# Three VectorE sums of x issued ahead of the weighting of v, with GpSimd busy beside them

## Chip, cores, metric

One core of a Trainium2 chip. The metric is device time in microseconds (us); lower is better.

## The reference

A linear ("performer") attention over eight batches, followed by a gated feed-forward layer, fp32 in and out:

```python
h = proj - sq; h = h - np.max(h, axis=-1, keepdims=True); phi = np.exp(h) / np.sqrt(m)
kv  = np.einsum('bhsm,bhsd->bhmd', k_p, v)          # with z = sum of k_p
num = np.einsum('bhsm,bhmd->bhsd', q_p, kv)         # attention = num / den
out = gelu(x @ w_gate) * (x @ w_val) @ w_out        # x: the attention, 4608 tokens x 512
```

## The kernel before

Each engine's instruction order is written by hand. While TensorE works on the feed-forward layer of one tile of 512 tokens, the attention of a later batch is prepared. The product with `w_val` uses seven products of half size in place of eight. It needs four sums of halves of the transposed x per tile (`ts`; they are coded as subtractions and called sums here). `v` multiplies v by weights that stand in for the subtracted maximum, in two halves; `kz` then multiplies k by it.

```python
def ts(self, n, eng):                      # class Gated; sum n of a token tile
    # ... cut: views b[row half, token half] of x, and t = x_sums
    p, q = ((b[0, 1], b[0, 0]), (b[1, 1], t[:, 0]), (b[1, 1], b[0, 1]), (b[1, 0], t[:, 1]))[n]
    eng.tensor_sub(t[:, n], p, q)          # two SBUF inputs, 128x512 bf16

def v(self, half, eng):                    # class Attention
    # ... cut: views
    eng.tensor_mul(vev[:, isl, :, :D], vfv[:, isl],
                   wkv[:, isl].unsqueeze(3).broadcast_to((P, NI // 2, 2, D)))   # two SBUF inputs, fp32
    eng.tensor_copy(vev[:, isl, :, D], wkv[:, isl])
```

The stretch in question (h is token tile 1, counted from zero; m is batch 2; n is batch 1):

```python
h.ts(0, nc.gpsimd)                                               # sum 0, on GpSimd
# ... cut
n.nx(4)
h.ga(0, 1)
after(load_kq("k", 3) + load_kq("q", 3) + load_v(3))             # three DMA issues, on GpSimd
m.qf(3, True)
h.ts(2, nc.vector)                                               # sum 2
m.qx(3)
h.vm(0, 1); h.vs(0, 1, act); m.kx(4); h.vm(0, 5)                 # P1, P5 on TensorE
h.ts(1, nc.vector)                                               # sum 1
m.v(1, pool)                                                     # v1, on GpSimd
m.v(0, nc.vector)                                                # v0
h.ga(6, 0); h.vm(0, 6); h.ga(6, 1)                               # P6
h.ts(3, nc.vector)                                               # sum 3
# ... cut: copies of ScalarE
h.vm(0, 7); h.va(0, 2); h.vm(0, 2)                               # P7, the addition that reads it, P2
h.gp(7, 0, 2); h.gp(7, 2, 4)
h.vm(0, 3); h.va(0, 1); h.vm(0, 4); h.va(0, 0)                   # P3, P4
h.ge(6)
m.kz(0, False); m.kz(1)                                          # kz, 72 small matmuls
```

The softmax here doesn't subtract the row's maximum and nothing guards it: scores larger than these inputs give would overflow.

## Time and profile before

| | before |
|---|---|
| time, median of 3 | 343.86 us (343.67 to 344.12) |
| TensorE busy | 96% of the span |
| TensorE idle, 68 to 75.3 us of the trace | 2.35 us |
| sum 3 on VectorE | 2.99 us, against 0.42 for its form |

TensorE sets the time, so what counts is the hole in its row near 73 us. The prediction shows the lines that carry this. The traces do not reach this stretch at the same time: sum 0 starts between 67.11 and 68.46 us, for reasons that lie ahead of the change (the traced run of the kernel before took 344.6 us). So I measure with D, the time from the start of sum 0 on GpSimd to the start of the tile product behind kz: before, 76.54 - 68.46 = 8.08 us.

### The profile page before, as it was taken

The numbers are of one execution on the slowest core, as the hardware profiler recorded it, in microseconds if no ns is written. First come the engines' busy times: TensorE is split into PE (matmuls) and PEld (weight loads), VectorE is DVE, ScalarE is ACT, GpSimd is POOL, SyncE is SP. The second block draws the span as 40 slices with busy tenths as digits, with TensorE's granted clock in tenths as the row PEclk, the third lists the DMA queues.
The fourth block names the chain that finished last, engine by engine and source line by source line (L and its number), as shares of the span: only waits on it lengthen the run. The fifth ranks groups of instructions, "written<-read, shape, count | busy, mean of one in ns | idle before, by whom it ended". The sixth has DMA issues, their size and how long they took to land.

```text
span 342.8 us, 7993 instructions
## 1 busy us (share of the span) xinstructions
PE 327.5 (96%) x3114; PEld 206.4 (60%) x3155; DVE 230.3 (67%) x479; ACT 214.3 (63%) x434; POOL 152.5 (44%) x154
## 2 busy tenths in 40 slices
PE   7889999879999999999999999999999999999994
PEld 3565455556645664476546654665476786686683
DVE  2975388879783759366836774567457677796783
ACT  3894366755687568756776577657765546626640
POOL 8326004073467446745594459476968400000000
PEclk9999999999999999999999999999999999999998
DMA  8999999599969454965298519772413041014004
GB/s 155 277 206 207 207 251 198 149 166 233 188 94 335 78 104 65 324 119 107 33 300 154 114 18 267 196 106 35 92 34 61 10 101 25 1 30 94 2 0 123
DMA packets 67173, 45.08 MB, mean 131 GB/s; under 512 B 47296, under 2 KB 60096, under 8 KB 67136
## 3 DMA queue, kind: packets, MB, share of 16 engines
q0 software_dynamic: 14848, 22.12, 31.3%
q1 hardware_dynamic: 51744, 21.64, 30.4%
q10 hardware_dynamic: 544, 0.82, 0.8%
q8 instruction: 24, 0.39, 0.5%
q14 instruction: 13, 0.11, 0.1%
HBM read 37.78 MB, written 9.44 MB: 138 GB/s over the span
## 4 chain that ended last, share of the span: by engine, by line
PE 83%; DVE 6%; DMA 3%; ACT 3%; issue 3%; POOL 2%; DVEq 0%; POOLq 0%
PE g_ps L433 20%; PE o_ps L559 17%; PE val_one L378 11%; PE val_two L378 9%; PE out_one L533 5%; PE out_two L533 3%; PE v_ps L462 3%; PE g_ps L425 3%; PE kz_ps L285 3%; DMA q_in<-in_q_dram 3%; PE nd L302 2%; PE pk L220 2%; DVE x_sb L314 2%; PE pq L242 2%; DVE val_c L387 1%
## 5 line engine op out<-in xcount | busy, mean ns | idle before, releaser
L433 PE MATMUL g_ps<-xT,w_gate_sb 128*128 128x512 bf16 x352 | 108.2, 379 | 0.5
L440 ACT ACTIVATE g_gelu<-g_ps 128x512 bf16<-128x512 f32 x108 | 63.6, 597 | 54.1 <-PE g_ps L433 25.3
L559 PE MATMUL o_ps<-w_out_sb,gated 128*128 128x512 bf16 x275 | 64.6, 380 | 1.1 <-issue 0.6
L480 POOL TENSOR_TENSOR gated<-g_gelu,val_c 128x512 bf16<-128x512 bf16 x29 | 33.7, 1164 | 50.8 <-DVE iden L313 26.2
L387 DVE TENSOR_TENSOR val_c<-val_one,val_c 128x256 f32<-128x256 f32 x48 | 20.3, 424 | 48.6 <-ACT g_gelu L440 39.6
L378 PEld LDWEIGHTS <-w_val_sb 128*128 128x128 bf16 x384 | 36.5, 98 | 18.3 <-issue 2.3
L559 PEld LDWEIGHTS <-gated 128*128 128x128 bf16 x288 | 26.5, 98 | 33.5 <-issue 3.9
L383 ACT COPY val_c<-val_one 128x256 f32<-128x256 f32 x95 | 35.2, 371 | 12.4 <-PE val_one L378 9.3
L249 ACT ACTIVATE q_pT<-pq 128x512 bf16<-128x512 f32 (+1 forms) x68 | 34.6, 598 | 11.9 <-PE pq L242 11.7
L378 PEld LDWEIGHTS <-val_sums 128*128 128x128 bf16 x288 | 27.3, 98 | 24.3 <-DVE x_sb L314 3.6
L233 DVE TENSOR_REDUCE nmax<-pk 128x8 f32<-128x1024 f32 (+2 forms) x43 | 39.7, 968 | 3.1 <-PE pk L220 1.2
L433 PEld LDWEIGHTS <-w_gate_sb 128*128 128x128 bf16 x376 | 34.9, 98 | 11.2
L378 PE MATMUL val_one<-x_sums,w_val_sb 128*128 128x256 bf16 x192 | 36.6, 273 | 1.7 <-DVE val_c L387 1.7
L228 ACT ACTIVATE k_p<-pk 128x1024 bf16<-128x1024 f32 (+2 forms) x43 | 33.0, 832 | 8.3 <-PE pk L220 6.7
L271 POOL TENSOR_TENSOR v_ext<-vf,wk 128x1152 bf16<-128x1152 f32 x13 | 30.3, 2334 | 14.0 <-ACT wk L260 14.0
L387 DVE TENSOR_TENSOR val_c<-val_two,val_c 128x256 f32<-128x256 f32 x96 | 36.0, 413 | 0.8 <-PE val_two L378 0.8
L484 POOL TENSOR_TENSOR gated<-g_gelu,val_c 128x256 bf16<-128x256 bf16 x34 | 24.2, 712 | 15.0 <-ACT g_gelu L440 15.0
L314 DVE TENSOR_TENSOR x_sb<-nd,iden 128x512 bf16<-128x512 f32 (+2 forms) x41 | 27.7, 676 | 1.4
L564 DVE COPY o_sb<-o_ps 128x512 f32<-128x512 f32 x20 | 13.7, 685 | 19.4 <-PE o_ps L559 14.9
L383 ACT COPY val_c<-val_two 128x256 f32<-128x256 f32 x45 | 16.8, 373 | 11.6 <-PE val_two L378 11.6
L484 DVE TENSOR_TENSOR gated<-g_gelu,val_one 128x256 bf16<-128x256 bf16 x48 | 20.0, 416 | 6.0 <-ACT g_gelu L440 5.7
L378 PE MATMUL val_two<-x_sums,val_sums 128*128 128x256 bf16 x96 | 18.4, 274 | 1.0 <-POOL x_sums L455 0.3
(104 smaller groups left out, 488.3 us busy)
## 6 DMA issues: line engine op xcount, KB each, us to landing
out_dram<-o_sb SPq DMA_DIRECT2D x67, 128.0 KB, 3.3
vf<-in_v_dram POOLq DMA_DIRECT2D x7, 1152.0 KB, 12.0
q_in<-in_q_dram POOLq DMA_DIRECT2D x8, 576.0 KB, 9.4
k_in<-in_k_dram POOLq DMA_DIRECT2D x7, 576.0 KB, 6.1
w_gate_sb<-in_moe_w_gate_dram POOLq DMA_DIRECT2D x3, 512.0 KB, 18.2
w_val_sb<-in_moe_w_val_dram POOLq DMA_DIRECT2D x3, 512.0 KB, 19.8
w_out_sb<-in_moe_w_out_dram POOLq DMA_DIRECT2D x3, 512.0 KB, 13.2
vf<-in_v_dram SPq DMA_DIRECT2D x1, 1152.0 KB, 5.7
```

What stands on the lines that cost most here:

```text
L228: last["begun"] = nc.scalar.activation(self.k_p[:, gs, i0:i0 + n, :], pk, func=Exp)
L233: nc.vector.reduce_max(self.nmax[:, gs, i0:i0 + n], pk, axis=AX, negate=True)
L249: last["begun"] = nc.scalar.activation(dst[:, a, i0:i0 + n], self.pq[c][a].rearrange("m (i e p) -> m i e p", e=2, p=SP), func=Exp)
L314: nc.vector.tensor_mul(x_sb[:n].rearrange("p (g h d) -> p g h d", g=2, h=4)[:, gs], ndv[:, :, :, :D], iden[:n, gs].broadcast_to((n, gs.sto ...
L378: nc.tensor.matmul(ps, w[:, c, self.i * P:(self.i + 1) * P], x[:, c], start=first and c == 0, stop=c == 1, skip_group_check=not first)
L383: copy(self.c[:, {1: 0, 6: 1, 5: 2}[n]], self.beta if n == 5 else self.one)
L387: nc.vector.tensor_add(part, (self.gamma, self.beta, self.one)[k], part)
L433: last["begun"] = nc.tensor.matmul(self.gps[jf], w_gate_sb[:, jm, jf * P:(jf + 1) * P], x_tiles[self.t][:, jm], start=(jm == 0), stop=(jm ...
L440: nc.scalar.activation(self.gelus[jf][:, part], src, func=Gelu)
L480: eng.tensor_mul(self.gated[:, i, :], self.gelus[i], self.v[i].row())
L484: eng.tensor_mul(self.gated[:, i + HF, ts], self.gelus[i + HF][:, ts], s.c[:, 2] if half else s.one)
L559: nc.tensor.matmul(self.ps[qq], self.g.gated[:, f, qq * P:(qq + 1) * P], w_out_sb[:, f, :], start=(jf == 0), stop=(jf == N_DFF - 1))
```

## The change

The intent: sum 3 loses 2.5 us behind v1. Issued ahead of v0 it would be through before v1 begins, and what waits for it would move up. No instruction is added or taken away.

```diff
         m.qf(3, True)
-        h.ts(2, nc.vector)
         m.qx(3)
 ...
         h.ts(1, nc.vector)
+        h.ts(2, nc.vector)
+        h.ts(3, nc.vector)
         m.v(1, pool)
         m.v(0, nc.vector)
         h.ga(6, 0)
         h.vm(0, 6)
         h.ga(6, 1)
-        h.ts(3, nc.vector)
```

## The prediction

> **Names.** Sum n is `h.ts(n)`, one 128x512 bf16 addition of halves of the transposed x of token tile 1 (counted from zero) into `x_sums`. Sum 0 runs on GpSimd, sums 1, 2 and 3 on VectorE. v0 and v1 are the halves of the weighting of v of batch 2, `m.v(0)` on VectorE and `m.v(1)` on GpSimd, each a multiply (line 271) and a small cast (line 273). P1 to P7 are the seven products `h.vm(0, n)` of TensorE. kz is `m.kz`, 72 small matmuls that read v0 in their first half and v1 in their second.
>
> **What bounds the kernel now.** First the page: the share of each engine, and the chain that ended last.
>
> ```profile
> PE 327.5 (96%) x3114; PEld 206.4 (60%) x3155; DVE 230.3 (67%) x479; ACT 214.3 (63%) x434; POOL 152.5 (44%) x154
> PE 83%; DVE 6%; DMA 3%; ACT 3%; issue 3%; POOL 2%; DVEq 0%; POOLq 0%
> ```
>
> TensorE is busy for 96% of the span and is 83% of the chain. So a change on VectorE is worth only what it takes out of a gap of TensorE. The next view, busy time by stretch, shows whether there is such a gap where the change works (columns: stretch, its length, busy time and instructions of PE, PEld, DVE, ACT, POOL, granted clock, DMA).
>
> ```profile
> core 0: us, PE busy (x) PEld busy (x) DVE busy (x) ACT busy (x) POOL busy (x), PEclk, DMA share, GB/s
> 68.00:75.30 7.30, 4.95 (x34) 2.87 (x36) 6.10 (x9) 4.34 (x8) 6.24 (x6) 1.00 0.85 139
> 75.30:94.00 18.70, 18.51 (x226) 12.96 (x230) 15.06 (x39) 9.82 (x22) 7.14 (x8) 1.00 1.09 214
> ```
>
> From 68 to 75.3 us TensorE misses 2.35 of 7.30 us; after that it misses 0.19 of 18.7. The chain of waits puts the largest hole behind sum 3:
>
> ```profile
> 71.73 0.26 DVE x_sums L455
> 71.99 2.51 issue
> 74.50 0.42 DVE val_c L387
> ```
>
> "issue" here is not real issue time: the timeline, in order of time (start, duration, engine, line, what, idle before and releaser), shows sum 3 lasting through it.
>
> ```profile
> 68.42 0.43 DVE L455 TENSOR_TENSOR x_sums<-xT 128x512 bf16<-128x512 bf16 x1 [0.16 <-DMA xT<-x_sb]
> 68.46 1.40 POOL L455 TENSOR_TENSOR x_sums<-xT 128x512 bf16<-128x512 bf16 x1 [10.55 <-DMA xT<-x_sb]
> 69.89 0.42 DVE L455 TENSOR_TENSOR x_sums<-xT,x_sums 128x512 bf16<-128x512 bf16 x1 [1.04 <-POOL x_sums L455]
> 70.23 1.35 DVE L271 TENSOR_TENSOR v_ext<-vf,wk 128x1152 bf16<-128x1152 f32 x1
> 71.58 2.99 DVE L455 TENSOR_TENSOR x_sums<-xT,x_sums 128x512 bf16<-128x512 bf16 x1
> 72.10 2.19 POOL L271 TENSOR_TENSOR v_ext<-vf,wk 128x1152 bf16<-128x1152 f32 x1
> 72.90 0.38 PE L378 MATMUL val_two<-xT,val_sums 128*128 128x256 bf16 x2
> 74.20 0.49 POOL L273 CAST v_ext<-wk 128x18 bf16<-128x18 f32 x1
> 74.50 0.41 DVE L387 TENSOR_TENSOR val_c<-val_one,val_c 128x256 f32<-128x256 f32 x1
> 74.97 0.38 PE L378 MATMUL val_one<-x_sums,w_val_sb 128*128 128x256 bf16 x2 [1.68 <-DVE val_c L387]
> 75.28 1.33 PE L285 MATMUL kz_ps<-v_ext,k_p 64*128 64x65 bf16 x72
> 76.54 0.39 PE L378 MATMUL val_one<-xT,w_val_sb 128*128 128x256 bf16 x2
> ```
>
> In order: sums 2, 0, 1, v0, sum 3 and v1; P3 at 72.90; the addition that reads P7 at 74.50; P4 at 74.97; kz; the next tile product at 76.54. Sum 3 takes 2.99 us, a sum of its form 0.42 (median of six). It stays open while v1 runs on GpSimd and ends 0.28 after v1's multiply does. Behind it in VectorE's queue stands the addition that P4 waits for (it frees the accumulator), and P4 stands in front of kz. So TensorE loses 1.68 us to a VectorE instruction whose own work is 0.4 us.
>
> **What the Trainium skill says.** "SBUF — State Buffer", section "Who interferes with whom": a VectorE instruction with two SBUF inputs contends with a GpSimd instruction that reads SBUF, as an exclusive lock; whoever issues first keeps it, and the other blocks for the whole instruction. The trace agrees in both directions: v1 blocks sum 3 (2.99 against 0.42), and sum 2, at 68.42, delays sum 0 on GpSimd (1.40 against a median of 1.15). The same pair v0/v1 of batch 1 collides the other way round, with VectorE first:
>
> ```profile
> 54.33 1.36 DVE L271 TENSOR_TENSOR v_ext<-vf,wk 128x1152 bf16<-128x1152 f32 x1
> 54.38 3.32 POOL L271 TENSOR_TENSOR v_ext<-vf,wk 128x1152 bf16<-128x1152 f32 x1 [10.93 <-ACT wk L260]
> 57.65 0.26 POOL L273 CAST v_ext<-wk 128x18 bf16<-128x18 f32 x1
> 18.68 0.75 PE L285 MATMUL kz_ps<-v_ext,k_p 64*128 64x65 bf16 x36 [0.23 <-POOL v_ext L273]
> ```
>
> GpSimd ends its multiply 2.01 us after VectorE's ends (57.70 less 55.69) and its cast 2.22 after. The VectorE cast in between took its usual 0.23. The last line, of batch 0, shows that the second half of kz waits for GpSimd alone, 36 matmuls after the first half had gone.[...] "Perfetto Trace Analysis", section "GPSIMD Engine Instruction", calls GpSimd spans unreliable. That fits: sum 3, free to begin at about 71.75, was already shut out although v1 is drawn from 72.10. So I take ends and spacings of GpSimd, not starts, as measures.
>
> **The change part by part.** The instruction order of the two kernels differs on VectorE alone: sum 2, sum 1, v0, sum 3 becomes sum 1, sum 2, sum 3, v0. Nothing is added or removed, and no engine gets more work. On TensorE one wait is new, of P7 for sum 2 (before it was covered by the wait for sum 1).
>
> (a) Sum 0 is no longer delayed: 1.40 becomes 1.15, so it ends at 69.61, not 69.86. The three DMA issues of GpSimd and v1 behind them come 0.25 earlier, v1 drawn from 71.85.
>
> (b) VectorE's sum 1 waits for sum 0 and starts 0.03 later, at 69.64; the place of sum 2 before it is now idle. Sums follow each other at 0.34 (69.89 to 70.23): sum 2 at 69.98, sum 3 at 70.32, v0 at 70.66. All three sums run while GpSimd only issues DMAs; sum 1 and v0 did so before without delay. v0 ends at 70.66 + 1.36 = 72.02, its cast at 72.16. P7 needs sum 2 at 71.55 and it is there at 70.4. P6 at 70.71 stays where it is, since a copy of ScalarE (70.28 + 0.38) releases it.
>
> (c) v1 asks for the lock while v0 holds it. By the spacing of batch 1 its cast ends 2.22 after 72.02, at 74.24, in place of 74.69.
>
> (d) The addition no longer stands behind a blocked sum 3. P7 is done at 71.93, the cast at 72.16, so the addition runs to about 72.55. P4 then needs no wait: it follows P3 at the usual 0.22, at 73.12. The first half of kz follows 0.31 later (74.97 to 75.28 before), at 73.43, and takes half of the 1.26 from 75.28 to 76.54, to 74.06. The second half needs v1: 74.24 + 0.06 = 74.30, and ends 0.63 later, at 74.93.
>
> (e) The next product starts at 74.93 in place of 76.54: 1.61 us saved. Without (a) it would be 0.25 less, 1.36.
>
> From there TensorE has 0.19 us of gaps up to 94 us, and each later step repeats at 35.46 us (pk at 129.22, 164.69, 200.15 in the chain). Its helpers wait for TensorE, not for a clock, so the saving should reach the end. I take 1.5 us, between the two sums: 343.86 - 1.5 = 342.4 us, or 0.4%.
>
> **Rivals.** First, the lock goes to v1 before v0: sum 3 was shut out 0.35 before v1's drawn start, so v1 claims early. Then v0 would be blocked until about 74.0, end at 75.4, and the addition, P4 and kz follow it: P4 at about 76, kz's end at about 77.5, some 1.0 us slower, 344.9. Against it: v0 starts at 70.66, and GpSimd still has its last DMA issue to begin at 71.08; before, v0 started at 70.23 in the same phase untouched. One in ten.
>
> Second, the wait for v1 takes the place of the wait for the addition, and all of kz waits for it: 74.30 + 1.26 = 75.56, a saving of 0.98, 342.9. Against it stands the batch 0 line above, and in the instruction list only the first matmul of the second half carries a wait for GpSimd.
>
> Third, the saving is given back at a transfer: loads for batch 3 and transposes of k do not get earlier by the same amount. The transposes of k are issued at 80.51 and land 7.0 later, at 87.5; the first reader runs at 93.74. That leaves 6 us, so I expect no loss. If it happened, 343.9.
>
> Fourth, new collisions of two-input VectorE work with GpSimd after 75 us, because the engines' phases move. They all follow TensorE, so their relative order should stay; I allow 0.3 us.
>
> **Range and chances.** The two sums give 342.25 and 342.5. The second rival and part losses reach 342.9 to 343.3, and little speaks for more than 1.9 us of gain, since the whole gap is 2.35. Before's three runs spread by 0.45. So 341.9 to 343.3 should hold eight times in ten, with the first rival outside it. Two per cent is 6.9 us, nearly three times the gap: within 2% is 0.98, and 0.01 each for faster and slower.
>
> **What would show each step.** (a) sum 0 near 1.15. (b) three VectorE sums of 0.42 in a row, then v0 of 1.36. (c) v1 lengthened, ending about 2.0 after v0. (d) P4 right behind P3, and kz in two pieces with a wait of some 0.2 for GpSimd. (e) the product after kz near 74.9, then 1.5 less at every later landmark, such as pk at 129.22. Wrong would be: v0 longer than 2 us, kz in one piece behind v1, or a landmark difference that shrinks between 75 and 130.

## The result, and the profile after

| | before | after |
|---|---|---|
| median, 4 runs each | 343.98 us | 345.68 us (345.17 to 346.27) |
| ratio | | 1.0051 (1.0032 to 1.0071) |
| D | 8.08 us | 8.84 us |
| TensorE idle, 68 to 75.3 us | 2.35 us | 2.68 us |

It is slower by 0.5%, within 2%, and outside the predicted range. The page's shares, then busy time by stretch:

```profile
PE 327.5 (95%) x3114; PEld 205.8 (60%) x3155; DVE 230.8 (67%) x479; ACT 214.3 (62%) x434; POOL 153.1 (45%) x154
PE 81%; DVE 8%; DMA 3%; issue 3%; ACT 2%; POOL 1%; SPq 0%; DVEq 0%; POOLq 0%
```

```profile
68.00:75.30 7.30, 4.62 (x32) 2.63 (x29) 6.23 (x7) 4.34 (x8) 6.80 (x6) 1.00 0.91 169
75.30:94.00 18.70, 18.51 (x221) 12.79 (x224) 15.06 (x40) 9.64 (x22) 7.14 (x8) 1.00 0.98 201
```

VectorE's share of the chain went from 6% to 8%; the hole in TensorE grew, and the stretch after it is as full as before. In the chain, "issue" now stands behind v0 in place of sum 3:

```profile
70.17 1.25 DVE v_ext L271
71.42 3.19 issue
```

The timeline of the changed kernel (start, duration, engine, line, what, idle before and releaser):

```profile
67.89 1.15 POOL L455 TENSOR_TENSOR x_sums<-xT 128x512 bf16<-128x512 bf16 x1 [10.50 <-DMA xT<-x_sb]
69.41 0.42 DVE L455 TENSOR_TENSOR x_sums<-xT 128x512 bf16<-128x512 bf16 x1
69.75 0.42 DVE L455 TENSOR_TENSOR x_sums<-xT,x_sums 128x512 bf16<-128x512 bf16 x1
70.08 4.61 DVE L271 TENSOR_TENSOR v_ext<-vf,wk 128x1152 bf16<-128x1152 f32 x1
71.28 2.19 POOL L271 TENSOR_TENSOR v_ext<-vf,wk 128x1152 bf16<-128x1152 f32 x1
73.39 1.42 POOL L273 CAST v_ext<-wk 128x18 bf16<-128x18 f32 x1
74.69 0.41 DVE L387 TENSOR_TENSOR val_c<-val_one,val_c 128x256 f32<-128x256 f32 x1
75.15 0.38 PE L378 MATMUL val_one<-x_sums,w_val_sb 128*128 128x256 bf16 x2 [2.44 <-DVE val_c L387]
75.46 1.33 PE L285 MATMUL kz_ps<-v_ext,k_p 64*128 64x65 bf16 x72
76.73 0.39 PE L378 MATMUL val_one<-xT,w_val_sb 128*128 128x256 bf16 x2
```

Sum 0 takes 1.15 and the sums 0.42, as predicted. But v0 takes 4.61 us in place of 1.36. It is drawn from 70.08 and ends 1.22 us after v1's multiply does (74.69 and 73.47), so most of its own 1.36 us ran only when v1 had done. v1 took the lock although it is drawn as starting 1.2 us after v0. The short sum 3, which v1 used to hold up, cost 0.28 us after v1's end; the long v0, with its cast, costs 1.22. GpSimd's cast is then caught by v0 in turn (1.42; undisturbed it takes 0.26). P4 waits 2.44 us, before 1.68.

Counted from the start of sum 0, D is 0.76 us longer; the time rose by 1.7. So a second cost had to be found.

A small part of it stands in this trace. Counted in the same way, the later landmarks lie 0.75 us behind those before up to pk at 164.87 us (before 164.69), but 1.04 behind at 200.62 (before 200.15). In the step between, an addition of VectorE waits 1.94 us, where it waits 1.58 in the four other steps that have it and in all five of the kernel before; the kernel before first, then the changed one:

```profile
180.01 0.42 DVE L387 TENSOR_TENSOR val_c<-val_one,val_c 128x256 f32<-128x256 f32 x1 [1.58 <-PE val_one L378]
180.55 0.43 DVE L387 TENSOR_TENSOR val_c<-val_one,val_c 128x256 f32<-128x256 f32 x1 [1.94 <-PE val_one L378]
```

The trace names no cause for these 0.29 us. They recur in after_again, e2, e3, e5 and e8 below, and as 0.38 in an earlier step of e4; the one trace of the kernel before, e1, e6 and e7 do not have them. Whether they belong to the change is not shown.

### The profile page after: what moved, and what is told of

Read it like the earlier page. It is cut to its first block, busy times and chain, and to the rows that moved or that the text cites. A ratio compares the mean times of both kernels' runs of the same rounds, so it can differ in the third digit from the quotient of the medians.

```text
span 343.3 us, 7994 instructions
## 1 busy us (share of the span) xinstructions
PE 327.5 (95%) x3114; PEld 205.8 (60%) x3155; DVE 230.8 (67%) x479; ACT 214.3 (62%) x434; POOL 153.1 (45%) x154
## 4 chain that ended last, share of the span: by engine, by line
PE 81%; DVE 8%; DMA 3%; issue 3%; ACT 2%; POOL 1%; SPq 0%; DVEq 0%; POOLq 0%
PE g_ps L433 20%; PE o_ps L559 16%; PE val_one L378 11%; PE val_two L378 9%; PE out_one L533 5%; PE out_two L533 3%; PE v_ps L462 3%; PE g_ps L425 3%; PE kz_ps L285 3%; DVE nmax L233 2%; PE nd L302 2%; PE pk L220 2%; DVE x_sb L314 2%; DMA kT<-k_in 2%; PE pq L242 2%
```

## The experiments

Nine runs; each kernel gave a correct result.

**after_again**: the changed kernel unaltered, for its time and clock.

> The changed kernel once more, for its time and to see whether its trace repeats. D is the time from the start of sum 0 on GpSimd to the start of the tile product behind kz: 8.08 us in the kernel before (68.46 to 76.54), 8.84 in the changed one (67.89 to 76.73). Theory (v1 claims the shared lock ahead of v0): D again 8.8, v0 again about 4.6 us long, time 0.8 to 1.7 us above the kernel before. Rival (the slower time comes from elsewhere, a later stage or the granted clock): D again 8.8, but the difference of the times well over 0.8, with a lower clock or a later landmark that drifts apart.

Measured: 346.06 us median of 6 (345.2 to 346.57) against 344.13, ratio 1.0056 (1.0043 to 1.0068). v0 is 4.62, D is 76.65 - 67.79 = 8.86. Its profiled run had a mean clock of 0.993; the first trace of the changed kernel had 1.0. Busy time by stretch shows where (the first number behind the POOL column is the granted clock):

```profile
76.00:77.00 1.00, 1.00 (x48) 0.87 (x41) 0.24 (x1) 0.00 (x0) 0.00 (x0) 0.84 1.69 88
77.00:78.00 1.00, 1.00 (x8) 0.70 (x6) 0.79 (x2) 0.71 (x2) 0.00 (x0) 0.50 1.08 172
78.00:79.00 1.00, 1.00 (x12) 0.80 (x11) 0.85 (x3) 0.66 (x2) 0.00 (x0) 0.50 1.21 242
79.00:80.00 1.00, 1.00 (x3) 0.30 (x2) 0.71 (x2) 0.37 (x1) 0.00 (x0) 0.50 1.07 426
```

For about 3.4 us (76.7 to 80.1) after the longer hole, TensorE runs at half clock. The chain of waits shows what that costs at the first matmuls of the next step, first in the changed kernel's first trace, then in this one:

```profile
93.99 0.78 PE pk L220 x24
```

```profile
95.34 0.78 PE pk L220 x24
```

From the start of sum 0 that is 26.10 and 27.55 us, so 1.45 us for the low clock; the kernel before has 93.81 - 68.46 = 25.35. The changed kernel's ten runs spread accordingly: the four with a mean clock of 1.0 took 345.17 to 345.39, the six with 0.992 to 0.995 took 345.74 to 346.57. The kernel before is not free of this: 3 of its 29 runs with a recorded clock had 0.993 and took 345.20 to 345.84, against about 344.1 for the others. None of these three was traced. Both theories of the expectation have a part: the lock (v0, D) and the clock.

**e1_sum2_early**: half of the change.

```diff
+        h.ts(2, nc.vector)      # ahead of m.qx(3), as before the change
 ...
         h.ts(1, nc.vector)
-        h.ts(2, nc.vector)
         h.ts(3, nc.vector)
```

> Only half of the change: sum 2 stays ahead of sum 1, as before, sum 3 goes ahead of v0. v0 then begins some 0.7 us after the end of sum 0 in place of 1.1. Theory (v1 claims the lock between 0.75 and 1.1 us after sum 0 has ended): v0 gets the lock first, takes 1.36, v1 ends about 2.0 after it, D 6.4 to 6.8, time 1.3 us below the kernel before. Rival (v1 claims the lock at once when sum 0 has ended, and single sums slip in between): v0 is blocked as in the changed kernel, about 4.6 us long, D about 8.8 to 9.1, time 0.8 us above.

Measured: 346.07 us against 344.13, ratio 1.0055 (1.0038 to 1.0073). The expectation missed: v0 was not let in first. Already sum 3 was shut out:

```profile
69.43 4.23 DVE L455 TENSOR_TENSOR x_sums<-xT,x_sums 128x512 bf16<-128x512 bf16 x1
```

Sum 3 reads what sum 1 writes, and is drawn 0.46 us after sum 1, not 0.34. That is 1.89 us after the start of sum 0 (67.54). In the changed kernel a sum drawn 1.86 us after it (69.75 - 67.89) was let through. Counted from the end of sum 0 the order would be the reverse (blocked at 0.49, let through at 0.71), because sum 0 takes 1.40 here; so I count from its start. D is 9.55, and the clock fell to 0.50 in this trace too.

**e3_v1_waits_v0**: the order on the lock is forced.

```diff
-        m.v(1, pool)
-        m.v(0, nc.vector)
+        v0 = m.v(0, nc.vector)
+        v1 = m.v(1, pool)
+        behind(v0[0], v1[:1])     # v1's multiply waits for v0's multiply
```

> The changed kernel with one more wait: v1 on GpSimd waits for the end of v0's multiply on VectorE, so that the order of the two on the lock is forced as the prediction assumed it. Theory (only who gets the lock first was wrong in the prediction): v0 1.36 us, v1 ends 2.0 to 2.2 later, kz in two pieces, D 6.5, time 1.3 to 1.6 us below the kernel before. Rival (GpSimd's DMA issues, not v1, block v0): v0 still over 2 us, until the third issue ends, D 7.5 or more.

Measured: 342.80 us median of 5 (342.14 to 343.13) against 344.13, ratio 0.9963 (0.9951 to 0.9975). Its timeline:

```profile
69.31 1.35 DVE L271 TENSOR_TENSOR v_ext<-vf,wk 128x1152 bf16<-128x1152 f32 x1
70.75 2.15 POOL L271 TENSOR_TENSOR v_ext<-vf,wk 128x1152 bf16<-128x1152 f32 x1 [0.24 <-DVE v_ext L271]
72.09 0.75 PE L285 MATMUL kz_ps<-v_ext,k_p 64*128 64x65 bf16 x36
73.16 0.76 PE L285 MATMUL kz_ps<-v_ext,k_p 64*128 64x65 bf16 x36 [0.32 <-POOL v_ext L273]
```

v0 takes 1.35, v1 ends 2.24 after it, kz goes in two pieces with a wait of 0.32, and D is 73.85 - 67.11 = 6.74: the predicted course, with 1.3 us gained. The DMA issues of GpSimd alongside v0 did not disturb it.

**e6_probe**: when is the lock taken? Fourteen tiny additions with two SBUF inputs stand behind sum 1.

```diff
         h.ts(1, nc.vector)
+        probe(14)        # 14 x nc.vector.tensor_add, 128x4 bf16, SBUF inputs
         h.ts(2, nc.vector)
```

> The changed kernel with 14 additions of 128x4 with two SBUF inputs between sum 1 and sum 2 on VectorE, as a probe of when the lock is taken (result unchanged, time not of interest). Theory: the probes run at their own pace, 0.1 to 0.2 us each, until some 0.75 to 1.1 us after the end of sum 0, and then one of them lasts until v1's multiply has ended, 2.5 us or more, although v1 is drawn as starting a microsecond later. Rival (only long operations are shut out, or the lock is taken when v1 is drawn as starting): all probes before v1's drawn start are short.

Measured: one look, 347.33 us, not of interest. Five probes follow each other at 0.07 us. The sixth:

```profile
69.90 3.73 DVE L137 TENSOR_TENSOR probe_sb<-still 128x4 bf16<-128x4 bf16 x1
```

It is drawn 1.88 us after the start of sum 0 (68.02) and 0.73 after sum 0's end, and ends when v1's multiply does (73.60). v1's multiply itself is drawn only from 71.41. So the lock was gone 1.5 us before the drawn start, and an operation of four elements per partition is shut out like a long one. Together with the runs above: let through at 1.86, blocked at 1.88 and 1.89. Here that is about when the first of three DMA issues ends (69.92); in e1 sum 3 was shut out 0.26 us before that (69.43, the issue ends at 69.69), so the end of an issue is not the mark.

**e4_v1_on_vector**: nothing on GpSimd that reads SBUF beside v0.

```diff
-        m.v(1, pool)
         m.v(0, nc.vector)
 ...
         h.va(0, 2)
+        m.v(1, nc.vector)
```

> The changed kernel with v1 moved from GpSimd to VectorE, behind v0 and the first addition: nothing on GpSimd then reads SBUF while v0 runs, though its three DMA issues stay where they were. Theory (v1's early claim of the lock, and nothing else of GpSimd, blocks v0): v0 1.36 us, v1 1.36, D 6.2 to 6.3, 1.7 to 1.9 us below the kernel before, some 0.4 faster than the kernel with the forced wait. Rival (descriptor generation itself blocks long two-input operations of VectorE): v0 over 2 us, D 7 or more.

Measured: 342.67 us (342.22 to 342.97) against 344.30, ratio 0.9949 (0.9935 to 0.9964). v0 and v1 take 1.35 each, D is 73.81 - 67.56 = 6.25, and kz goes in one piece at 72.54. So it is v1 on GpSimd, not the DMA issues alone, that blocks v0. Both this kernel and e3 beat the two kernels. By D this one is 0.5 us ahead of e3, but the intervals of their times overlap.

**e8_after_filled**: the changed kernel with TensorE's hole filled.

```diff
         h.va(0, 1)                        # cut: kz then keeps this accumulator
+        m.kz_ps = two_banks("kz_ps", False)
+        for _ in range(10): nc.tensor.matmul(m.kz_ps[0][0], still[:, :P], still)
         h.vm(0, 4)
```

> The changed kernel with ten dummy matmuls of 128x512 in TensorE's gap ahead of P4, written into the accumulator of kz, which kz then overwrites. Theory (the slower ones of the changed kernel's runs come from the granted clock, which falls to 0.50 for 3 to 4 us after the longer gap): the clock stays at 1.00 from 75 to 84 us, D about 8.8 to 9.0, and all runs lie at 345.0 to 345.5, none near 346.4; median 1.1 us above the kernel before. Rival (the two groups of runs have another cause): the runs still fall into two groups 1 us apart, median 1.7 above.

Measured: 345.38 us median of 6 (344.75 to 345.63) against 344.30, ratio 1.0025 (1.0010 to 1.0040). D is 8.84, so the lock costs as much as ever, but no run lies near 346.4, all six have a mean clock of 0.998 or more, and the clock stays up in the trace:

```profile
77.00:78.00 1.00, 1.00 (x22) 0.72 (x15) 0.71 (x2) 0.40 (x2) 0.00 (x0) 1.00 2.16 126
78.00:79.00 1.00, 0.96 (x14) 0.67 (x13) 1.00 (x4) 1.00 (x3) 0.00 (x0) 1.00 0.72 116
```

Useless matmuls made the changed kernel faster, by 0.31% in the two ratios (1.0056 to 1.0025), or 1.1 us. What is left, 0.25% or 0.9 us (0.3 to 1.4), fits the 0.76 us that D grew by and the 0.29 lost later.

**e7_probe_two_issues**: the probe kernel with one DMA issue fewer between sum 0 and v1.

```diff
-        after(load_kq("k", 3) + load_kq("q", 3) + load_v(3))
+        after(load_kq("k", 3) + load_kq("q", 3) + load_v(3, nc.sync))
```

> The probe kernel with the load of v for batch 3 issued from SyncE, so that two DMA issues, not three, stand between sum 0 and v1 on GpSimd (time not of interest). Sums and probes so far fit one moment of the claim, 1.87 us after the start of sum 0 (let through at 1.86, blocked at 1.88 and 1.89). Theory A[...]: the first blocked operation starts about 0.5 to 0.75 us earlier, 1.1 to 1.4 after the start of sum 0. Theory B (the claim comes a fixed time after sum 0, whatever stands between): a probe at about 1.88 is the first blocked. In both the blocked one ends with v1's multiply, now 0.75 us earlier.

Measured: one look, 347.29 us, not of interest. Sum 1, 1.19 us after the start of sum 0 (67.94), goes through; the very first probe, at 1.53, is blocked:

```profile
69.47 3.33 DVE L137 TENSOR_TENSOR probe_sb<-still 128x4 bf16<-128x4 bf16 x1
```

So the claim comes between 1.19 and 1.53, 0.33 to 0.69 us earlier for one issue fewer. Theory B is out. A's direction holds, but the blocked probe lies outside the 1.1 to 1.4 that it named (the claim itself may lie inside), and the step per issue is smaller than an issue's drawn 0.75 us.

**e2_sum2_late**: the other half of the change.

```diff
         h.ts(1, nc.vector)
         h.ts(2, nc.vector)
-        h.ts(3, nc.vector)
 ...
         h.ga(6, 1)
+        h.ts(3, nc.vector)
```

> The other half of the change: sum 2 goes behind sum 1, but sum 3 stays behind v0 as before. v0 is then drawn from 1.86 us after the start of sum 0, just ahead of the claim at 1.87. Theory (claim at 1.87 us): v0 gets the lock by a hair, 1.36 us, sum 3 is blocked as in the kernel before, D 7.9 to 8.1, time within 0.3 us of the kernel before. If v0 loses by a hair: v0 about 4.6, D 9.0 or more, time 1 to 2 us above.

Measured: 344.54 us against 344.30, ratio 1.0003 (0.9987 to 1.0019). v0 got in by a hair, 1.86 us after the start of sum 0:

```profile
69.78 1.36 DVE L271 TENSOR_TENSOR v_ext<-vf,wk 128x1152 bf16<-128x1152 f32 x1
```

Sum 3 was then blocked as in the kernel before (2.66 us), and D is 75.75 - 67.92 = 7.83. The claim time found from the other runs foretold this. D is 0.25 us shorter and the time is not, since this trace too loses 0.29 us between 165 and 200 us.

**e5_loads_behind_v1**: no DMA issue between sum 0 and v1.

```diff
-        after(load_kq("k", 3) + load_kq("q", 3) + load_v(3))
+        begun3 = last["begun"]
 ...
         m.v(1, pool)
+        behind(begun3, load_kq("k", 3) + load_kq("q", 3) + load_v(3))
         m.v(0, nc.vector)
```

> The changed kernel with the three DMA issues for batch 3 moved behind v1 on GpSimd, so that v1 follows sum 0 directly. Theory[...]: with no issue between, the claim comes at once after sum 0 and lasts only v1's own time; the blocked VectorE operation (sum 1 or sum 2) takes 2.2 to 2.7 us, not 4.2 to 4.6, v0 is free with 1.36, D 7.8 to 8.2, time within 0.4 us of the kernel before. Rival (the length of the block has nothing to do with the issues): the blocked operation still takes over 4 us and D is 9 or more.

Measured: 344.29 us against 344.04, ratio 1.0001 (0.9969 to 1.0033). v1 now follows sum 0 directly and catches sum 1, for 2.35 us in place of 4.2 to 4.6; v0 takes 1.35. D is 75.34 - 67.75 = 7.59, a little under the expected 7.8. So the length of the block depends on the issues that v1 has ahead of it.

## Why the prediction was wrong

**What bounds the kernel: right.** TensorE, with a hole behind a blocked VectorE operation. Its stretch from 75.3 to 94 us stayed equally full, and in the first trace the later landmarks carried the difference on, with 0.29 us added between 165 and 200 us.

**(a) and the sums of (b): right.** Sum 0 took 1.15, all three sums 0.42, and P6 and P7 found them ready. For sum 3 this was luck: it came 1.86 us after the start of sum 0, and in the probe run an operation at 1.88 was shut out.

**v0 in step (b), with (c): the step that failed.** I let v0 start at 70.66 "untouched" because GpSimd still had its last DMA issue to begin at 71.08. That took the claim to come after the last issue. The runs put it about 1.87 us after the start of sum 0, near the end of the first of three issues. In the prediction's own frame that is 68.46 + 1.87 = 70.33, and v0 came at 70.66. v1's lead over its drawn start, which I read off sum 3 as "0.35", was only a lower bound: sum 3 had merely been the first to knock. The probe shows 1.5 us. My counter-evidence, the v0 before at 70.23, fitted because it lay 1.77 us after sum 0's start, 0.1 us ahead of the claim.

**(d) and (e): wrong as a consequence, right once v0 goes first.** With the forced wait P4 follows P3 directly, kz splits and 1.3 us are gained, against 1.5 predicted. D is 6.74 where I had 6.47 (74.93 - 68.46). So the mechanism of the gain was right and the winner of the lock wrong.

**The first rival happened, and I gave it one in ten.** Its size was near for the lock alone: D of 9.04 by its numbers (77.5 - 68.46), measured 8.84. Its 344.9 missed the clock.

**The clock was in no step and no rival.** The hole grew to 2.44 us, and in six of ten runs the mean clock was lower; in the one of them that was traced TensorE ran at 0.50 for about 3.4 us, which cost 1.45 us. "TensorE: Matmul & The Clock Gate" (the Trainium skill), section "What's actually happening", gives a window of 3413 ns that runs freely and lets the clock fall after an idle window. The length of the low phase agrees, and a free-running window fits that only some runs are hit. In the clock records of the packed traces the low phase lasts 3.413 us in all four traces that have one, and the full clock before it lasted 71.68 us in two and 68.27 in two, which are 21 and 20 such lengths. But a hole of 2.45 us, shorter than the window, was enough in after_again, and one of 2.44 in the first trace was not. Filling the hole removed the slow group (none of six runs, against six of ten), so the cause is shown.

**The sum.** 0.76 us from the lock, 0.29 from the later wait, and 1.45 in six of ten runs (0.87 on average) give an estimate of 1.9; measured were 1.7 and 1.9 in the two comparisons. The 0.29 has no shown cause.

**Still open.** Why v1 claims that early. "Perfetto Trace Analysis" (the Trainium skill), sections "GPSIMD Engine Instruction" and "DMA Instruction — SWDGE (GPSIMD)", says that GpSimd is eight cores with queues of their own, that descriptors are generated on two of them, and that the drawn start is core 0's. The other six could then begin v1, and hold the lock, while two still issue. That the claim and the length of the block move with the number of issues fits this, but no record of single cores shows it, and the step per issue (0.33 to 0.69 us) is not explained. The claim time itself rests on drawn starts 0.02 us apart in different traces.

## What to carry to other kernels

When VectorE and GpSimd both run operations with two SBUF inputs, treat the order in which they get the shared lock as something to be fixed by a dependency, or put both on one engine; issue order and the drawn GpSimd starts do not tell who wins, above all when DMA issues stand ahead of the GpSimd operation. When you move a short operation out of a block, ask which operation takes its place there, and how long that one is. And a TensorE gap that grows towards 2.5 us can cost more than its own length, through the clock (1.45 us more in the trace read).

## What the Trainium skill lacked or had wrong

- "SBUF — State Buffer": whoever issues first keeps the lock. Here v0, drawn 1.20 us ahead of v1, lost it (4.61 us). The page lacks that a GpSimd operation queued behind DMA issues claims up to 1.5 us before its drawn start.
- "SBUF — State Buffer": the block is as long as the other instruction. Here it was longer, and began while GpSimd was still drawn issuing DMAs: 3.73 us for a probe, with a v1 of 2.19; 2.35 for a sum with no issue between.
- "Perfetto Trace Analysis": calls GpSimd spans unreliable, without a size; 1.5 us here.
- "TensorE: Matmul & The Clock Gate": its rule warns of idle gaps over about 3 us. Here the clock fell to 0.50 after gaps of 2.45 and 3.03 us, not after one of 2.44, and not after 1.68 and 1.43 in the traces seen; but 3 of 29 runs of the kernel with 1.68 had a lower mean clock (0.993), untraced.
